# Seven added order constraints and one changed priority in the planner of an attention and two-MoE kernel

## The chip, the cores and the metric

The kernel runs on one core of a Trainium2 chip. Its engines are PE (the matmul array), DVE (vector), ACT (scalar), POOL (GpSimd) and SP, whose queue issues most of the DMAs. Each engine works through its own list of instructions in order, and waits at an instruction until what it needs is there. The metric is the device time of one execution in microseconds, and the time before is the median of 3 runs.

## The reference

Three stages follow each other. `B` is 4 batches, `H` 8 heads, `S` 576 tokens, `D` 64, `M` 32 memory slots.

```python
a = exp(phi - max(phi, axis=2)); a = a / (sum(a, axis=2) + 1e-09)     # over the 32 slots
k_m, v_m = einsum('bhsm,bhsd->bhmd', a, k), einsum('bhsm,bhsd->bhmd', a, v)
attn = softmax(q @ k_m.T / 8); x = (attn @ v_m), laid out as [2304 tokens, 512]

logits = x @ w_gate; e_idx = argmax(logits)                           # first MoE: 8 experts, one per token
out[mask_e] = gate_w * sigmoid(x @ w_output_gate)[:, e] * (relu(x @ w1[e]) @ w2[e])

p = domain_probs / (sum(domain_probs) + 1e-09)                        # second MoE: all 4 experts
out = sum_e p[:, e] * (relu(x @ w1[e]) @ w2[e])
```

## The kernel before

The attention is cut into eight units, u0 to u7: two of them (four heads each) per batch. A unit's steps have names that its instructions' lines tell: `ldph`, `ldkv`, `ldq` load phi, keys and values, and q; `mx` (lines 399 to 401, DVE) is the maximum over phi, `tr`, `gm`, `dg`, `pm` (L410, L417, L422, L426) turn it into one maximum per slot, `sub` (L432) subtracts it, `exp` (L440) follows on ACT, `es` on POOL and `pe` (L468) add up, `kva` and `kvb` (L449) are the products with keys and values, `r`, `kd`, `vd`, `vl` (L478 to L517) scale them, `ktT` (L502) and `kt` transpose, `sc0` and `sc1` (L569) are the scores, `t0` to `aT` (L594 to L634) the softmax, and `x0`, `x1` (L678) the output, which is split into a high and a low part (L686, L689 and others).

When both units of a batch are done, `route` (r0 to r3) computes the logits (L738), the largest one (`lz`), counts how many tokens chose each expert (`pc`, L812) and makes the most frequent expert's number (`idx`, lines 819 to 829, DVE). SP reads that number (`start`, L835, a TENSOR_LOAD) and loads that expert's weights (L1084). They are split on ACT (L1094) and DVE (L1102), and the dense matmuls of the first MoE begin (L942, then L950): batch 0's first one is the operation `m0a0`. From there on attention steps of later units stand between dense matmuls. Tokens that chose another expert are counted in `left` (L874) and would be handled in a general loop at the end. The second MoE (L1483, L1538) follows from about 300 us on, and its weights per token, `pr`, are loaded by `ld_probs` (L309, L313: 19 small DMAs in seven operations) and normalized by `probs` (L324 to L327, DVE).

What sets the order of all this up to the second MoE is a planner, `Plan`, which runs when the kernel is built. Each operation has an engine, an estimated cost, a priority (lower goes first), operations that it needs, and buffers that it takes. `run` steps through an imagined time, lets each engine take the ready operation of best priority, and writes its instructions at once, so that the order in which operations are taken becomes the order on each engine for good. An operation in `next` of another only has to be taken after that other one was; an operation in `succ` has to wait for its end. Until `m0a0` is taken, an idle PE is given `fill`, a 128 x 128 matmul of ones (L1361, named warm). Three of the lines that matter here:

```python
UNIT_PRIO = (158, 150, 200, 228, 230, 420, 656, 270)
        ld_probs.append(op(f"ld_probs{i0}", "S", 1.5, 650.0, [])(f))
    @op("probs", "V", 0.9, 1500.0, ld_probs)
```

Of the kernel before, what the change touches and what calls it, by code (L numbers as in the profile page):

```python
# [32 lines left out]
class Plan:  # L33
# [8 lines left out]
    def op(self, name, eng, cost, prio, after=(), take=()):  # L42
        def add(fn):
            o = Op(name, eng, cost, fn, prio, [(x,) if isinstance(x, str) else x for x in take])
            for a in after:
                if isinstance(a, tuple):
                    o.need += 1
                    a[0].next.append(o)
                elif a is not None:
                    o.need += 1  # L50
                    a.succ.append(o)
            self.ops.append(o)
            return o

        return add
# [101 lines left out]
def attn_moe_moe_kernel(  # L157
# [63 lines left out]
    left = const.tile([1, B], F32, name="left")  # L221
# [33 lines left out]
    plan = Plan(caps)  # L255
# [464 lines left out]
    def route(b, pri):  # L720
# [3 lines left out]
        def o(name, eng, cost, after=(), take=(), dp=0.0):  # L724
            return op(n0 + name, eng, cost, pri + dp, after, take)
# [115 lines left out]
        dp = 280.0  # L841
# [27 lines left out]
            T["pn"] = bank2(pn.got[0], "pn")[:, 0]  # L869
            nc.tensor.matmul(T["pn"][0:1, 0:1], T["ci"], ones[:P, 0:1], start=True, stop=True)  # L870

        @o("left", "V", 0.07, [pn], [], dp)
        def lf():
            nc.vector.tensor_scalar(left[:, b:b + 1], T["pn"][0:1, 0:1], -1.0, float(S), op0=ALU.mult, op1=ALU.add)  # L874

        plan.free(pn, 0, lf)

        @o("gate", "V", 2.12, [eo, oh], [], dp)
# [23 lines left out]
        def keep():  # L902
            nc.sync.dma_start(out=rs_d[b], in_=rest[b].rearrange("p j e -> p (j e)"))

        att_done.extend((start, gate, cb, lf, oh, eo))

    def w1_srcs(w1, e, nf):
# [512 lines left out]
    def first_w1(u, after, prev):  # L1420


        @op(f"n{u}t", "G", 3.6, pw_ - 500.0, [wraws_[2 * u], prev])
        def t():
            W0[u] = raw_tile(ts_p, "ts")
            for f in t_ops(wraws[(1, u)], W0[u]):
                f(nc.gpsimd)

        @op(f"n{u}h", "A", 2.2, pw_ - 500.0, [t, after])
        def h():  # L1430
            W1[u] = [big.tile([128, NP * 256], F32R, tag="xb", name="w") for _ in range(2)]
            for part in w1_parts(wraws[(1, u)], W0[u]):
                w1_hi(W1[u][0], part)

        @op(f"n{u}l", "G", 4.8, pw_ - 500.0, [h])
        def l():
            for part in w1_parts(wraws[(1, u)], W0[u]):
                w1_lo(nc.gpsimd, *W1[u], part)

        plan.free(wraws_[2 * u], 0, l)  # L1440
        return l

    n0l = first_w1(0, done_l1[2], None)
    first_w1(1, done_l1[3], n0l)
    plan.free(warm, 0, next(o for o in plan.ops if o.name == "m0a0"))
    plan.run()

    mctx.close()
# [190 lines left out]
```

## Time and profile before

| | |
|---|---|
| median of 3 runs | 1057.53 us (1056.83 to 1058.07) |
| profiled execution: its time, and its span | 1060.37 us, 1058.5 us |
| busy share of PE, DVE, POOL, ACT | 98%, 53%, 49%, 35% |
| granted PE clock, mean | 0.996 of full speed |
| first dense matmul (L942) | 54.94 us from the span's start |

The span is what the profiler saw between the first and the last instruction, and the time contains what lies around it as well. Busy time is what instructions take on an engine; a busy PE is not necessarily a PE at its full rate, which is why the granted clock is shown beside it.

### The profile page before, as it was taken

The numbers are of one execution on the slowest core, as the hardware profiler recorded it, in microseconds if no ns is written. First come the engines' busy times: TensorE is split into PE (matmuls) and PEld (weight loads), VectorE is DVE, ScalarE is ACT, GpSimd is POOL, SyncE is SP. The second block draws the span as 40 slices with busy tenths as digits, with TensorE's granted clock in tenths as the row PEclk, the third lists the DMA queues.
The fourth block names the chain that finished last, engine by engine and source line by source line (L and its number), as shares of the span: only waits on it lengthen the run. The fifth ranks groups of instructions, "written<-read, shape, count | busy, mean of one in ns | idle before, by whom it ended". The sixth has DMA issues, their size and how long they took to land.

```text
span 1058.5 us, 15693 instructions
## 1 busy us (share of the span) xinstructions
PE 1041.5 (98%) x6210; PEld 947.8 (90%) x6210; DVE 556.1 (53%) x1014; ACT 365.8 (35%) x610; POOL 519.3 (49%) x518
## 2 busy tenths in 40 slices
PE   8999999999999999999999999999999999999997
PEld 7879898999999999999998999999998999999996
DVE  4888876747334444545464454544456453453533
ACT  2343342424423243333243234333333323323330
POOL 1110110000447666766666665776666666666550
PEclk9999999999999999999999999999999999999999
DMA  9999883535442122212214212212214221221201
GB/s 197 171 237 183 156 256 79 184 89 185 136 144 80 45 76 80 65 56 80 80 50 129 80 40 81 80 47 74 80 51 129 80 69 51 80 80 40 60 20 63
DMA packets 137954, 104.93 MB, mean 99 GB/s; under 512 B 37008, under 2 KB 119952, under 8 KB 137872
## 3 DMA queue, kind: packets, MB, share of 16 engines
q1 hardware_dynamic: 137424, 102.66, 36.1%
q0 software_dynamic: 448, 1.19, 0.5%
q8 instruction: 50, 0.82, 0.3%
q14 instruction: 32, 0.26, 0.1%
HBM read 84.87 MB, written 18.96 MB: 98 GB/s over the span
## 4 chain that ended last, share of the span: by engine, by line
PE 91%; DMA 3%; DVE 3%; ACT 1%; SPq 1%; issue 0%
PE po L1538 37%; PE ab L1483 32%; PE p L942 9%; PE p L950 8%; DMA ph<-in_phi_dram 2%; DMA kv<-in_v_dram 1%; PE ub L449 1%; PE warm L1361 1%; PE px L678 1%; PE pss L569 1%; DVE l L1493 1%; PE pl L738 0%; DVE acc L1522 0%; PE pl L768 0%; ACT h L1492 0%
## 5 line engine op out<-in xcount | busy, mean ns | idle before, releaser
L1483 PE MATMUL ab<-zo,w 128*128 128x384 f32 x2004 | 401.4, 335 | 3.1 <-DVE zo L1286 3.1
L1483 PEld LDWEIGHTS ab<-zo,w 128*128 128x128 f32 x2004 | 356.2, 188 | 30.9 <-DVE zo L1286 3.7
L1538 PE MATMUL po<-w,h 128*128 128x512 f32 x1152 | 372.9, 391 | 0.3 <-ACT h L1492 0.3
L1538 PEld LDWEIGHTS po<-w,h 128*128 128x128 f32 x1152 | 214.4, 188 | 29.1 <-ACT h L1492 0.6
L1538 PE MATMUL po<-w,l 128*128 128x512 f32 x576 | 225.6, 392 | 0.0
L1344 POOL TENSOR_TENSOR w<-ts,w 128x512 fp32r<-128x512 f32 x92 | 118.4, 1308 | 127.3 <-ACT w L1568 127.3
L1492 ACT ACTIVATE h<-ab 128x384 fp32r<-128x384 f32 x143 | 70.3, 492 | 261.6 <-DVE ab L1514 170.9
L1344 POOL TENSOR_TENSOR w<-raw,w 128x512 fp32r<-128x512 f32 x100 | 102.8, 1050 | 112.9 <-ACT w L1340 112.9
L1493 DVE SCALAR_TENSOR_TENSOR l<-ab,h 128x384 fp32r<-128x384 f32 x143 | 79.8, 558 | 140.5 <-ACT h L1492 140.5
L1506 DVE TENSOR_TENSOR u<-ab,s 128x384 f32<-128x384 f32 x96 | 53.5, 558 | 150.9 <-PE ab L1483 119.0
L1573 POOL TENSOR_TENSOR w<-raw,w 128x512 fp32r<-128x512 f32 x96 | 123.9, 1310 | 16.4 <-ACT w L1563 16.4
L1538 PEld LDWEIGHTS po<-w,l 128*128 128x128 f32 x576 | 108.1, 188 | 16.6 <-DVE l L1493 0.3
L942 PE MATMUL p<-x,w 128*128 128x288 f32 x768 | 109.1, 299 | 0.0
L942 PEld LDWEIGHTS p<-x,w 128*128 128x128 f32 x768 | 104.0, 190 | 2.5 <-issue 2.1
L950 PE MATMUL p<-hh,w 128*128 128x288 f32 x512 | 93.6, 299 | 0.0
L1492 ACT ACTIVATE h<-t 128x384 fp32r<-128x384 f32 x48 | 25.2, 526 | 166.9 <-DVE t L1511 166.9
L1327 POOL TENSOR_TENSOR ts<-raw 128x256 f32<-128x256 f32 x92 | 81.8, 889 | 1.2 <-DMA raw<-in_moe_w_dram 1.2
L1493 DVE SCALAR_TENSOR_TENSOR l<-t,h 128x384 fp32r<-128x384 f32 x48 | 67.4, 1404 | 28.4 <-ACT h L1492 28.4
L950 PEld LDWEIGHTS p<-hh,w 128*128 128x128 f32 x512 | 76.2, 189 | 1.8 <-issue 1.7
L1327 POOL TENSOR_TENSOR ts<-raw,ts 128x256 f32<-128x256 f32 x92 | 68.7, 746 | 3.6
L1511 DVE TENSOR_TENSOR t<-ab,u 128x384 f32<-128x384 f32 x47 | 26.2, 557 | 62.5 <-PE ab L1483 62.5
L1514 DVE TENSOR_TENSOR ab<-ab,u 128x384 f32<-128x384 f32 x95 | 53.0, 558 | 6.5 <-PE ab L1483 6.4
(150 smaller groups left out, 906.3 us busy)
## 6 DMA issues: line engine op xcount, KB each, us to landing
raw<-in_moe_w_dram SPq DMA_DIRECT2D x79, 512.0 KB, 3.9
raw<-in_moe_w_dram SPq DMA_DIRECT2D x98, 256.0 KB, 4.3
xs<-x SPq DMA_DIRECT2D x16, 576.0 KB, 6.0
kv<-in_k_dram SPq DMA_DIRECT2D x16, 288.0 KB, 6.1
kv<-in_v_dram SPq DMA_DIRECT2D x16, 288.0 KB, 6.7
zs<-z SPq DMA_DIRECT2D x8, 576.0 KB, 5.2
ph<-in_phi_dram SPq DMA_DIRECT2D x8, 288.0 KB, 6.0
qt<-in_q_dram SPq DMA_DIRECT2D x16, 144.0 KB, 7.1
```

The costliest lines, as they stand in the source:

```text
L942: nc.tensor.matmul(pp[:, n, :HS], w[wi][:, kk, fs], zz[:, kk, n * HS:(n + 1) * HS], start=(kk == 0 and m == 0), stop=(kk == KD_ - 1 and m ...
L950: nc.tensor.matmul(pp[:, n, :HS], w[wi][:, j, :], hx[:, n * HS:(n + 1) * HS], start=(f == 0 and wi == 0 and hx is hh), stop=(f == NF - 1 a ...
L1327: lambda eng, o_=o_, x=x, y=y: eng.tensor_tensor(o_, x, y, op=ALU.subtract)
L1344: eng.tensor_tensor(wl[:, sl], src, wh[:, sl].bitcast(F32), op=ALU.subtract)
L1483: nc.tensor.matmul(p, w[:, s], z[:, zi, kk], start=(k not in (2, 3, 6) and kk + n == 0), stop=(kk == 1 and n == 2), skip_group_check=True,)
L1492: nc.scalar.activation(a, p, ACTF.Relu)
L1493: nc.vector.scalar_tensor_tensor(c, p, 0.0, a.bitcast(F32), op0=ALU.max, op1=ALU.subtract)
L1506: nc.vector.tensor_tensor(sums[n], p, sums["s1"], op=ALU.add)
L1511: nc.vector.tensor_tensor(t, p, sums["u3"], op=ALU.add)
L1514: nc.vector.tensor_tensor(p, p, sums["u3" if k == 5 else "u2"], op=ALU.add)
L1538: nc.tensor.matmul(po[t], hx[:, s], w[:, 1024 * wi + 512 * a:1024 * wi + 512 * a + 512], start=(i == 0 and a + n == 0), stop=(i == NI - 1 ...
L1573: nc.gpsimd.tensor_tensor(w[:, 1024:][:, c], wraws[(2, u)][:, c], w[:, c].bitcast(F32), op=ALU.subtract)
```

## The change

The priority of `left` goes from that of the rest of its group to the front, and seven pairs are added: the second name of each pair may be taken by the planner only after the first was. The pairs hold `u2mx` and the cast of the gates' weights (`gates`, L319 and L320) until `u1vd` has been taken, `u2sub` until `u1sb2`, `u3mx` until `u1aT`, `u4mx` until `r0idx`, the second q transpose of unit u1 until `u1pe`, and `r0pn` until `m0a0`. Costs, other priorities, buffers and the computation stay as they are.

```diff
@@ -869,7 +869,7 @@
-        @o("left", "V", 0.07, [pn], [], dp)
+        @o("left", "V", 0.07, [pn], [], -20.0)
         def lf():
@@ -1443,6 +1443,19 @@
     plan.free(warm, 0, next(o for o in plan.ops if o.name == "m0a0"))
+
+    named = {o.name: o for o in plan.ops}
+    for x, o in (
+        ("u1vd", "u2mx"),
+        ("u1vd", "gates"),
+        ("u1sb2", "u2sub"),
+        ("u1aT", "u3mx"),
+        ("r0idx", "u4mx"),
+        ("u1pe", "u1qt1"),
+        ("m0a0", "r0pn"),
+    ):
+        named[x].next.append(named[o])
+        named[o].need += 1
     plan.run()
```

The planner makes of it a different order from the second unit on. On DVE, around the index of route 0 (L819 to L829), there stood before (`lz`, `lmx`, `oh` are the logits, their maximum and the choice; `gm` and `dg` belong to units u3 and u4; `idx` is the expert's number):

```order
L751 TENSOR_REDUCE lz<-pl 96x96
L804 TENSOR_REDUCE lmx<-lz 96x6
L806 TENSOR_TENSOR oh<-lz,lmx 96x48
L417 TENSOR_REDUCE gm<-ub 128x1
L859 TENSOR_TENSOR dl<-lz,lmx 96x48
L422 TENSOR_SCALAR dg<-ident,gm 128x128
L417 TENSOR_REDUCE gm<-ub 128x1
L819 TENSOR_REDUCE cnt<-pc 128x8
L823 TENSOR_REDUCE cmx<-cnt 128x1
L825 SCALAR_TENSOR_TENSOR sel<-cnt,cmx,prio 128x8
L828 TENSOR_REDUCE cmx<-sel 128x1
L829 TENSOR_SCALAR idx_94<-cmx 1x1
```

Now there stands, at the same place:

```order
L804 TENSOR_REDUCE lmx<-lz 96x6
L806 TENSOR_TENSOR oh<-lz,lmx 96x48
L859 TENSOR_TENSOR dl<-lz,lmx 96x48
L324 TENSOR_REDUCE prs<-pr 128x18
L325 TENSOR_SCALAR prs<-prs 128x18
L326 RECIPROCAL prs<-prs 128x18
L327 TENSOR_TENSOR pr<-pr,prs 128x72
L819 TENSOR_REDUCE cnt<-pc 128x8
L823 TENSOR_REDUCE cmx<-cnt 128x1
L825 SCALAR_TENSOR_TENSOR sel<-cnt,cmx,prio 128x8
L828 TENSOR_REDUCE cmx<-sel 128x1
L829 TENSOR_SCALAR idx_94<-cmx 1x1
```

The steps of u3 and u4 have left this place, and the four instructions of `probs`, which before came after route 1, stand ahead of the counts. On SP, ahead of the read of the index (`TENSOR_LOAD idx`), before:

```order
L389 DMA ph<-in_phi_dram 96x4x192
L359 DMA qt<-in_q_dram 96x6x64 x2
L336 DMA kv<-in_k_dram 96x2x384
L337 DMA kv<-in_v_dram 96x2x384
L313 DMA pr<-in_moe_domain_probs_dram 96x4
L313 DMA pr<-in_moe_domain_probs_dram 32x4
L313 DMA pr<-in_moe_domain_probs_dram 64x4 x2
L313 DMA pr<-in_moe_domain_probs_dram 32x4
L313 DMA pr<-in_moe_domain_probs_dram 96x4
L352 DMA qd<-in_q_dram 32x18x32 x4
L835 TENSOR_LOAD idx_94
```

And now, at the same place:

```order
L313 DMA pr<-in_moe_domain_probs_dram 96x4 x2
L313 DMA pr<-in_moe_domain_probs_dram 32x4
L313 DMA pr<-in_moe_domain_probs_dram 64x4 x2
L313 DMA pr<-in_moe_domain_probs_dram 32x4
L313 DMA pr<-in_moe_domain_probs_dram 96x4
L309 DMA pr<-in_moe_domain_probs_dram 128x9x4
L336 DMA kv<-in_k_dram 96x2x384
L337 DMA kv<-in_v_dram 96x2x384
L359 DMA qt<-in_q_dram 96x6x64 x2
L835 TENSOR_LOAD idx_94
```

All 19 small loads of `pr` now come ahead of the read, in one row (before, 12 of them did, in two groups), and phi and the keys of u4 and the first q load of u4 have moved behind it. On PE, at the start of the dense matmuls (L942), before:

```order
L1361 MATMUL warm<-ones 128x128 x2
L449 MATMUL ub<-kv,ph 32x128 x12
L1361 MATMUL warm<-ones 128x128
L449 MATMUL ub<-kv,ph 32x128 x12
L1361 MATMUL warm<-ones 128x128 x2
L468 MATMUL ub<-ones,es 128x1
L1361 MATMUL warm<-ones 128x128 x2
L942 MATMUL p_807<-x,w 128x288 x24
L942 MATMUL p_855<-x,w 128x288 x12
L449 MATMUL ub<-kv,ph 32x128 x12
L942 MATMUL p_855<-x,w 128x288 x12
```

And now:

```order
L1361 MATMUL warm<-ones 128x128 x3
L426 MATMUL ub<-dg,ones 96x128
L1361 MATMUL warm<-ones 128x128 x9
L942 MATMUL p_785<-x,w 128x288 x24
L870 MATMUL pn<-ones,ci 1x1
L942 MATMUL p_826<-x,w 128x288 x12
L449 MATMUL ub<-kv,ph 32x128 x12
L942 MATMUL p_826<-x,w 128x288 x12
L449 MATMUL ub<-kv,ph 32x128 x12
```

The two L449 groups ahead of L942 before are those of u3, and the one behind it is u4's; now both groups behind L942 are u3's, and u4's come later. Ahead of the dense start stand 91 fillers, where 75 stood.

## Rows read from the trace of the kernel before

**Rows 1.** The page: share and instructions of PE; one kind of DMA issue, us to landing.

```profile
PE 1041.5 (98%) x6210; PEld 947.8 (90%) x6210; DVE 556.1 (53%) x1014; ACT 365.8 (35%) x610; POOL 519.3 (49%) x518
...
qt<-in_q_dram SPq DMA_DIRECT2D x16, 144.0 KB, 7.1
```

**Rows 2.** Table by stretches: length, busy us per engine, PE clock, DMA share, GB/s.

```profile
60.50:63.00 2.50, 0.03 (x2) 0.03 (x1) 1.67 (x3) 1.59 (x2) 0.00 (x0) 1.00 1.12 287
...
64.25:68.00 3.75, 3.75 (x36) 2.98 (x34) 2.85 (x6) 2.83 (x4) 0.00 (x0) 0.54 0.84 134
...
150.00:300.00 150.00, 150.00 (x1161) 145.34 (x1160) 84.96 (x159) 52.14 (x78) 19.33 (x20) 1.00 0.42 134
```

**Rows 3.** PE's timeline: start, us, instruction, count, idle before it and its releaser.

```profile
26.45 0.30 PE L410 MATMUL ub<-ident,mx 96*128 96x96 f32 x1 [1.15 <-DVE mx L401]
...
49.46 1.53 PE L1361 MATMUL warm<-ones 128*128 128x128 f32 x12
...
54.94 5.25 PE L942 MATMUL p<-x,w 128*128 128x288 f32 x36
...
63.01 0.85 PE L449 MATMUL ub<-kv,ph 96*32 96x128 f32 x20 [2.48 <-DMA kv<-in_v_dram]
```

**Rows 4.** SP's timeline of DMA issues: start, us until the last is issued, count.

```profile
31.58 1.24 SPq L359 DMA_DIRECT2D qt<-in_q_dram  x2
...
38.06 0.33 SPq L336 DMA_DIRECT2D kv<-in_k_dram  x1
...
51.02 3.50 SPq L1084 DMA_DIRECT2D raw<-in_moe_w_dram  x4
54.61 0.45 SPq L336 DMA_DIRECT2D kv<-in_k_dram  x1
...
96.83 5.61 SPq L313 DMA_DIRECT2D pr<-in_moe_domain_probs_dram  x6
```

**Rows 5.** The chain in order of time, 50 to 55 us: start, us, what.

```profile
50.99 0.42 PE ub L426 x2
...
51.87 0.79 PE ub L449 x24
...
54.51 0.13 PE ub L468 x2
```

**Rows 6.** SP's waits, 0 to 110 us: total, times, longest.

```profile
SPq L313 <- DMA qt<-in_q_dram: 1.6, 2, 1.2
```

**Rows 7.** Lines L313 and L309: ns of an issue (min/median/max); L309's landing.

```profile
L313 SPq DMA_DIRECT2D pr<-in_moe_domain_probs_dram x18: 317/490/1502, 32.9 to 102.0; - x18
...
DMA to landing us min/median/max: 2.7/2.7/2.7
```

**Rows 8.** DVE's timeline, columns as in PE's.

```profile
39.63 0.12 DVE L478 TENSOR_SCALAR rs<-ub 128x1 f32<-128x1 f32 x1
...
40.90 0.86 DVE L517 SCALAR_TENSOR_TENSOR vl<-ub,rm,vd 128x64 fp32r<-128x64 f32 x4
...
46.84 0.21 DVE L819 TENSOR_REDUCE cnt<-pc 128x8 f32<-128x48 f32 x1
...
47.74 0.14 DVE L829 TENSOR_SCALAR idx<-cmx 1x1 int32<-1x1 f32 x1
...
49.03 0.48 DVE L594 STREAM_TRANSPOSE t<-pss 128x288 f32<-128x288 f32 x1 [1.15 <-PE pss L569]
...
50.66 0.24 DVE L422 TENSOR_SCALAR dg<-ident,gm 128x128 f32<-128x128 f32 x1
...
70.72 0.20 DVE L846 TENSOR_TENSOR oh<-oh,prio 96x48 f32<-96x48 f32 x1
...
71.81 0.20 DVE L854 TENSOR_REDUCE ci<-inp 96x1 f32<-96x48 f32 x1
...
144.61 0.23 DVE L324 TENSOR_REDUCE prs<-pr 128x18 f32<-128x72 f32 x1
...
145.38 0.23 DVE L327 TENSOR_TENSOR pr<-pr,prs 128x72 f32<-128x72 f32 x1
```

## The prediction

> **What bounds the kernel now.** I read the page's shares first: PE is busy 98% of the span [rows 1]. So only three things can move the end: when the dense matmuls begin, how much other matmul work then shares PE with them, and the time PE stands still or runs slow behind that point. The table by stretches gives the last: from 150 to 300 us PE is busy throughout, while from 60.5 to 63 it is almost idle, and from 64.25 to 68 its granted clock averages 0.54 [rows 2]. PE's timeline names the places: the first dense matmul (L942) starts at 54.94, and at 60.5 the product of keys and values of the fifth unit, u4 (L449), waits 2.48 us for a kv load [rows 3]. That load was issued at 54.61, behind four loads of expert weights [rows 4]. After its 2.48 us of standing still PE fell from 2.4 to 1.2 GHz for most of 3.75 us; at 0.54 this cost 3.75 x 0.46 = 1.72 us.
>
> **What the change does, by engine.** The seven pairs only hold an operation back in the plan; at run time they add no wait themselves. But the plan is one program, so it shifts everything near the front.
>
> *PE behind the dense start.* Before, four units have their keys-and-values product ahead of the first L942 and five units their maxima; in the changed order it is three and four. One unit's two L449 groups (0.79 us each), an L426 (0.42), an L468 (0.13) and an L410 (no dearer than that; I take 0.08) move behind the start: 2 x 0.79 + 0.42 + 0.13 + 0.08 = **+2.2 us** [rows 5]. No cover: PE is full there.
>
> *The stall at 60.5.* Now the L449 behind 36 dense matmuls belongs to the fourth unit; its kv and q loads stand ahead of the expert weights in SP's order, issued at about 44 where PE needs them at about 61. I take the stall and its slow clock as gone: -2.48 - 1.72 = **-4.2 us**. Ends: 0 (it moves to another unit) and -4.2; the value taken is that of the kv load being early.
>
> *The dense start.* This is the uncertain term. The plan costs a `ld_probs` operation at 1.5 us, but its six small loads took 5.61 us on SP at 96.83 [rows 4]. The changed SP order issues all 19 before route 0's index is read, and the `probs` sums (L324 to L327), which wait for all of them, now stand on DVE directly ahead of the counts that make that index (L819 to L829). DVE is in order, so a normalization needed only hundreds of microseconds later sits in the chain that starts the dense work. Working forward:
> SP is unchanged up to the sixth small load. The seventh takes the place of the kv load at 38.06 [rows 4]. SP's small loads also wait for the end of earlier transfers, as for a q load [rows 6], but the last bulk load ahead of them is issued at 31.58 [rows 4] and lands within about 7 us [rows 1], so that from 39 on they run alone. A small load holds SP 0.49 us in the median [rows 7]: twelve from 38.06 give 38.06 + 11 x 0.49 = 43.45 for the issue of the last, and its landing took 2.7 us [rows 7]: 46.15. With the issue of the nineteenth I take **46.5**.
> DVE should be at L324 by about 44: it counted at 46.84 before, with the maxima of two more units ahead. So the landing decides.
> From 46.5: the four `probs` instructions, 144.61 to 145.61, 1.0; the five of the index, 46.84 to 47.88, 1.04; that is 48.55, against 47.88 before [rows 8]. Behind it the sums of the third unit, u2, kd, vd, vl (39.63 to 41.76, 2.13), six of the one-hot count (70.72 to 72.01, 1.29), two L594 (0.48 each, overlapping to about 0.4), L417 and L422 (0.24 each): 1.3 [rows 8]. This is 53.25; L426 on PE with its handover, 0.5; then nine fillers that stand in PE's order before L942, at 0.25 each (six, of two passes each, took 1.53 at 49.46 [rows 3]), 2.25. Together 48.55 + 2.13 + 1.29 + 1.3 + 0.5 + 2.25 = 56.0. The weights do not decide: their first load can issue at about 49.3, before 51.02 [rows 4]. So the start moves from 54.94 to 56.0: **+1.1 us**. Ends: if the loads land at 45 and DVE and PE keep step, -0.4; if each issue takes 5.61 / 6 = 0.94 us, the last is issued at 48.4, lands at 51.1, and the start moves +5.7.
>
> *Sum:* 2.2 - 4.2 + 1.1 = **-0.9 us**. On the profiled execution's span, 1058.5 becomes 1057.6. Its own time is 1060.37, 2.84 above the median of 1057.53; the same difference on the median gives **1056.6 us**. A change of 0.2% (2.1 us) is about what measurement tells from nothing here, so the forecast is no measurable change.
>
> **Rivals.**
> *The clock falls before the dense start (0.25).* In the changed order PE runs out of work at about 47.2 (fillers behind the last q transposes) and next needs the third unit's kd, some 0.8 us behind the index: 2.15 us idle. An idle of 1.15 us at 25.3 left the clock whole [rows 3], 2.48 us at 60.5 did not [rows 2, 3]. Half clock over the 2 to 4 us of PE's work ahead of L942 adds 1 to 2 us: sum +0.1 to +1.1, so 1057.6 to 1058.6. The Trainium skill, "TensorE: Matmul & The Clock Gate", Part 1 (the HAM clock gate), says that an idle array falls to half rate and needs sustained work to come back; by that rule the fillers pay, and the trace's fall at 64.25 agrees.
> *Slower: the small loads are slow (0.13).* At 0.94 us per issue the start moves +5.7 and the sum is +3.7: 1061.2. For it: 5.61 us for six at 96.83, and one issue of 1.50 us [rows 4, 7]; against it: those stood beside streams of q loads, and here no bulk runs. It decides (+2.1) once the last small load lands at 49.5 or later.
> *The stall stays (0.08).* The fourth unit's exponential stands on ACT behind the casts of the second and third weight pieces. If the third lands 2 us late, PE waits for it and its clock falls again: the 4.2 us come back, sum +3.3, 1060.8. For it: the exponential would end about 1 us before PE asks. Against: the weights are issued 1.7 us earlier with less ahead of them.
> *Faster: the loads are no wait (0.14).* If the 19 land by 44, the index is ready at 46 and the start at 53.5, sum -3.4: 1054.1. This is what the reordering by itself gives (two units' maxima off DVE ahead of the first softmax). For it: an issue can take 0.317 us [rows 7]: 11 x 0.32 from 38.06 is 41.6, landing 44.3. Against: back-to-back issues there took more.
>
> **How the numbers follow.** The forecast itself has 0.40. Faster by over 0.2%: all of the last rival, and 0.08 of the forecast for a landing near 45: 0.22. Slower: the slow loads, the stall that stays, and 0.03 of the clock rival: 0.24. The rest is 0.54. The range takes in both sides' cases, 1053.8 to 1061.2, leaving about 2 in 10 outside.
>
> **What would show it.** In the new trace: L324 waiting for a probs load, ending at 46 to 47; L829 at about 48.5; first L942 at 55.5 to 56.5; no L449 waiting for kv at 60 to 62; a granted clock of 1.00 from the start of L942 on; no PE wait over 1 us between 56 and 300. It is wrong if L324 ends before 45 or after 49.5, if the clock is at half when L942 begins, or if a new wait stands in the first 20 us of the dense work.

## The result: 1.4% slower, and the profile after

The changed kernel took 1074.64 us (median of 4 runs, 1071.10 to 1077.94); the kernel before, beside it on the same chip, 1057.80 (4 runs). The ratio is 1.0139, 95% interval 1.0114 to 1.0163. The profiled execution took 1077.94 us with a span of 1076.2 us, against 1060.37 and 1058.5: 17.7 us more span.

Four rows of PE's timeline answer to [rows 3] (start, us, instruction, idle before it and its releaser):

```profile
50.00 0.47 PE L502 MATMUL ub<-ident,kd 128*128 128x128 f32 x1 [1.84 <-DVE vl L517]
...
57.70 3.44 PE L942 MATMUL p<-x,w 128*128 128x288 f32 x24
...
91.53 0.59 PE L468 MATMUL ub<-ones,es 96*128 96x1 f32 x2 [6.36 <-POOL es L401]
...
153.14 0.42 PE L410 MATMUL ub<-ident,mx 96*128 96x96 f32 x1 [3.29 <-DVE mx L401]
```

The dense start is at 57.70, not 54.94. The wait for keys and values at 60.5 is gone, but two new ones stand behind the start: 6.36 us for u4's `es`, the sums that POOL makes, and 3.29 us for the maxima of u7. The table by stretches answers to [rows 2] (length, busy us of PE, PEld, which loads PE's weights, DVE, ACT and POOL, then PE clock, DMA share, GB/s):

```profile
50.00:54.00 4.00, 4.00 (x18) 2.42 (x18) 1.00 (x6) 0.89 (x3) 0.00 (x0) 0.60 0.92 302
57.70:85.10 27.40, 27.40 (x279) 24.83 (x277) 25.31 (x54) 13.69 (x20) 4.11 (x4) 1.00 1.13 188
85.10:91.50 6.40, 0.08 (x1) 0.00 (x0) 0.23 (x1) 0.00 (x0) 2.48 (x4) 0.67 1.02 162
91.50:99.00 7.50, 7.46 (x40) 7.47 (x41) 4.07 (x11) 0.96 (x2) 0.00 (x0) 0.60 1.10 295
149.80:153.20 3.40, 0.12 (x2) 0.06 (x1) 1.24 (x4) 0.00 (x0) 0.00 (x0) 0.85 1.08 324
153.20:162.00 8.80, 8.80 (x62) 7.37 (x63) 6.91 (x12) 3.23 (x5) 3.46 (x4) 0.67 0.51 190
```

Behind each idle stretch the granted clock is at its lower level, 1.2 of 2.4 GHz, for some microseconds: 7.50 x 0.40 = 3.0 us lost behind the first new wait, 8.80 x 0.33 = 2.9 us behind the second. These terms add up to nearly all of the 17.7: dense start 57.70 - 54.94 = 2.8; the deferred unit's work, 2.2 as forecast; 6.36 + 3.0 and 3.29 + 2.9 for the waits; 1.1 for two small waits at 271 and 275; less the 4.2 of before's own stall: 17.5. They compare one execution with one, not the medians.

The first new wait comes from an engine that the prediction never read. POOL's timeline before (its columns are those of PE's):

```profile
59.00 1.32 POOL L401 TENSOR_TENSOR es<-treeG 96x128 f32<-96x128 f32 x1
78.00 0.88 POOL L897 DMA_DIRECT2D cfd<-cf  x1 [17.68 <-DVE cf L891]
87.89 0.58 POOL L898 DMA_DIRECT2D cbc<-cfd  x1 [9.01 <-DMA cfd<-cf]
109.45 1.64 POOL L399 TENSOR_TENSOR treeG<-ph 96x384 f32<-96x384 f32 x1 [20.98 <-ACT ph L440]
```

And after:

```profile
63.37 0.65 POOL L401 TENSOR_TENSOR es<-treeG 96x128 f32<-96x128 f32 x1
74.11 0.88 POOL L897 DMA_DIRECT2D cfd<-cf  x1 [10.09 <-DVE cf L891]
88.83 0.58 POOL L898 DMA_DIRECT2D cbc<-cfd  x1 [13.84 <-issue]
89.42 1.00 POOL L399 TENSOR_TENSOR treeG<-ph 96x384 f32<-96x384 f32 x1
90.50 0.45 POOL L400 TENSOR_TENSOR treeG<-treeG 96x128 f32<-96x128 f32 x1
91.03 0.45 POOL L401 TENSOR_TENSOR es<-treeG 96x128 f32<-96x128 f32 x1
```

Before, u4's `es` (59.00) comes ahead of route 0's two gate DMAs: L897 writes 2.2 KB of gate values to memory, L898 reads them back to all partitions (the broadcast), and has to wait until they are there. After, `es` of u4 stands behind both (91.03 is u4's, 63.37 is u3's). Its input has been ready since ACT's exponential ended at 80.73, but POOL stands at L898 for 13.84 us, then needs 2.06 us for the three instructions of `es`, and PE, whose next instruction is L468, waits there. The planner had put the two DMAs at 6.0 us; from the start of L897 to the end of L898 they took 15.3 here (10.5 before). The orders on POOL differ at one more place, since route 1's broadcast now comes ahead of u5's `es` too, but no PE wait at L468 came of that in this kernel. The Trainium skill, "DMA: Bandwidth & Descriptors", section "Anatomy of one DMA", says that a DMA's wait on a semaphore is done by the sequencer that issues it; L898 agrees, with POOL held for 9.01 us before and 13.84 after. By the same section's fit (2.0 us and a term for bytes) 2.2 KB would land in about 2 us, which is an estimate; the view of DMA issues shows five times that, and the measurement decides (KB each, median us to landing):

```profile
cfd<-cf POOLq DMA_DIRECT2D x4, 2.2 KB, 10.2
```

### The profile page after: what moved, and what is told of

Same layout as the page of the kernel before. It is cut to its first block, busy times and chain, and to the rows that moved or that the text cites. A ratio compares the mean times of both kernels' runs of the same rounds, so it can differ in the third digit from the quotient of the medians.

```text
span 1076.2 us, 15760 instructions
## 1 busy us (share of the span) xinstructions
PE 1048.3 (97%) x6242; PEld 953.7 (89%) x6242; DVE 556.6 (52%) x1014; ACT 365.6 (34%) x610; POOL 518.4 (48%) x518
## 4 chain that ended last, share of the span: by engine, by line
PE 88%; DMA 3%; DVE 3%; SPq 2%; issue 2%; ACT 0%; POOL 0%; DVEq 0%; POOLq 0%
PE po L1551 36%; PE ab L1496 31%; PE p L950 9%; PE p L942 8%; DMA qt<-in_q_dram 1%; DMA cfd<-cf 1%; SPq L359 1%; DMA ph<-in_phi_dram 1%; PE pss L569 1%; PE ub L449 1%; SPq L313 1%; PE warm L1361 1%; PE px L678 1%; DVE l L1506 1%; DVE acc L1535 0%
## 5 line engine op out<-in xcount | busy, mean ns | idle before, releaser
L1519 DVE TENSOR_TENSOR u<-ab,s 128x384 f32<-128x384 f32 x96 | 53.5, 558 | 151.0 <-PE ab L1496 119.0
L942 PE MATMUL p<-x,w 128*128 128x288 f32 x768 | 113.3, 304 | 1.1 <-DVE z L1193 1.0
L942 PEld LDWEIGHTS p<-x,w 128*128 128x128 f32 x768 | 106.5, 194 | 5.5 <-issue 3.8
L897 POOL DMA_DIRECT2D cfd<-cf x4 | 3.2, 790 | 128.5 <-DVE cf L891 79.7
```

The source lines that it names most:

```text
L942: nc.tensor.matmul(pp[:, n, :HS], w[wi][:, kk, fs], zz[:, kk, n * HS:(n + 1) * HS], start=(kk == 0 and m == 0), stop=(kk == KD_ - 1 and m ...
L1519: nc.vector.tensor_tensor(sums[n], p, sums["s1"], op=ALU.add)
```

## The experiments

Theory 1: PE waits because POOL, in order, stands at route 0's broadcast with u4's `es` behind it; the half clock behind the wait is its consequence. Theory 2: u3 and u4 as a whole are too late, by the late dense start and by their held maxima, and this wait is only where it shows. Theory 3, for the second wait: SP's order issues u7's phi too late.

The results first. The span, the dense start, PE's idle time behind it and the time lost to the lower clock behind it (up to 300 us; summed over slices of 1 us of the table by stretches, the loss as busy time times one minus the clock) are of the one profiled execution.

| kernel | median, and before beside it | ratio, 95% | span | dense start | idle | lost to clock |
|---|---|---|---|---|---|---|
| before | 1057.80 | | 1058.5 | 54.94 | 3.1 | 1.7 |
| changed | 1074.64 / 1057.80 | 1.0139 (1.0114 to 1.0163) | 1076.2 | 57.70 | 11.3 | 5.9 |
| 1: es ahead of broadcast | 1068.76 / 1058.71 | 1.0077 (1.0054 to 1.0101) | 1069.4 | 60.65 | 5.2 | 1.7 |
| 2: before, es behind broadcast | 1066.03 / 1058.71 | 1.0062 (1.0035 to 1.0090) | 1064.2 | 56.17 | 6.7 | 3.4 |
| 3: probabilities later | 1071.30 / 1058.71 | 1.0104 (1.0073 to 1.0135) | 1071.4 | 53.53 | 10.2 | 6.9 |
| 4: only u3, u4 pairs | 1072.77 / 1058.71 | 1.0127 (1.0094 to 1.0160) | 1069.7 | 57.90 | 9.5 | 3.4 |
| 5: es and phi | 1066.69 / 1061.16 | 1.0060 (1.0037 to 1.0083) | 1064.1 | 54.73 | 5.3 | 3.4 |
| 6: es, phi, probabilities | 1063.58 / 1061.16 | 1.0035 (1.0014 to 1.0056) | 1059.8 | 53.25 | 4.7 | 0.0 |
| 7: broadcast planned at 15 | 1080.51 / 1061.16 | 1.0169 (1.0137 to 1.0200) | 1083.2 | 60.47 | 14.2 | 6.5 |
| 8: only u2 pairs | 1084.50 / 1061.16 | 1.0227 (1.0199 to 1.0256) | 1079.9 | 56.23 | 16.1 | 7.3 |
| 9: fillers ahead of L502 | 1075.73 / 1060.43 | 1.0146 (1.0104 to 1.0187) | 1070.7 | 56.22 | 10.8 | 2.2 |
| 10: fourth pair, z | 1065.63 / 1060.43 | 1.0048 (1.0022 to 1.0073) | 1063.6 | 53.72 | 6.5 | 1.7 |
| 11: before, u4's product held | 1069.58 / 1060.43 | 1.0080 (1.0053 to 1.0106) | 1063.8 | 56.01 | 7.3 | 2.5 |
| 12: before, kv load on ACT | 1061.55 / 1060.43 | 1.0008 (0.9983 to 1.0033) | 1064.0 | 59.22 | 4.4 | 1.7 |

One column has to be read with care. With the same instructions up to it, the dense start differs from execution to execution: 57.70, 60.65, 54.73 and 60.47 us in the changed kernel's order (changed, 1, 5, 7), 54.94, 56.17, 56.01 and 59.22 in that of before (before, 2, 11, 12). These ranges overlap, so a difference of 2.8 us between two executions says little of the medians.

**1. u4's `es` ahead of the broadcast.** The changed kernel with one more pair:

```diff
         ("m0a0", "r0pn"),
+        ("u4es", "r0cbc"),
```

> The changed kernel with one more pair: route 0's cbc (the two gate DMAs on POOL) may be taken only after u4's es. Every other queue keeps its order. Theory 1 (POOL's order): L401 of u4 no longer stands behind L898, the wait of 6.36 us at L468 and the 3.0 us of half clock behind it go, so about 9.4 us less: 1065 us. Theory 2 (u3 and u4 are late as a whole): another PE wait of 3 us or more takes the place of this one within 15 us, and the gain stays under 4 us: above 1070.

POOL's timeline and PE's, of this kernel:

```profile
85.55 0.46 POOL L401 TENSOR_TENSOR es<-treeG 96x128 f32<-96x128 f32 x1
85.95 0.88 POOL L897 DMA_DIRECT2D cfd<-cf  x1
97.93 0.58 POOL L898 DMA_DIRECT2D cbc<-cfd  x1 [11.10 <-DMA cfd<-cf]
```

```profile
50.14 0.47 PE L502 MATMUL ub<-ident,kd 128*128 128x128 f32 x1 [1.98 <-DVE vl L517]
...
60.65 1.56 PE L942 MATMUL p<-x,w 128*128 128x288 f32 x10
...
146.88 0.30 PE L410 MATMUL ub<-ident,mx 96*128 96x96 f32 x1 [3.18 <-DVE mx L401]
```

The broadcast waits as long as ever (11.10 us), but nothing of PE's stands behind it: no wait at L468 is left, nor its half clock, and no wait over 0.6 us took its place until the one at 146.88. Theory 2 asked for one of 3 us within 15 us, and falls for this wait. Only POOL's order differs from the changed kernel's, at this one place. The median fell by 5.9 us, the ratio from 1.0139 to 1.0077, with intervals that do not overlap: less than the 9.4 expected. In the profiled execution half clock ahead of the dense start lasted much longer (60.65 against 57.70 with the same instructions up to there); why the median gained less is not shown.

**2. The swap alone, in the kernel before.**

```diff
+    named = {o.name: o for o in plan.ops}
+    for x, o in (
+        ("r0cbc", "u4es"),
+    ):
+        named[x].next.append(named[o])
+        named[o].need += 1
     plan.run()
```

> The kernel before with one pair: u4's es may be taken only after route 0's cbc. None of the seven pairs of the change is in it, and the way to the dense start is the same. Theory 1: route 0's broadcast ends near 88.5 us, es ends near 90.6, PE is at L468 near 84.5, so a wait of about 6 us and some 3 us of half clock: 9 us or more slower than before, 1066 to 1072. Theory 2 (the swap is harmless without late u3 and u4): within 2 us of before.

```profile
61.13 1.35 PE L449 MATMUL ub<-kv,ph 96*32 96x128 f32 x24
...
86.91 0.38 PE L468 MATMUL ub<-ones,es 96*128 96x1 f32 x2 [2.29 <-POOL es L401]
...
130.95 0.38 PE L468 MATMUL ub<-ones,es 96*128 96x1 f32 x2 [1.68 <-POOL es L401]
```

PE's timeline shows the wait, twice (the planner then put route 1's broadcast ahead of u5's `es` too), each with half clock behind it; the kernel is 7.3 us slower by the medians. None of the change's pairs is needed for the wait. It is smaller than expected, since the first broadcast came 4 us earlier here (L898 at 83.83). Not all of the 7.3 us is the swap's: the planner moved later work too, and three waits for `hl` (the low part of the hidden layer, L962) of 2.6 us together stand at 262 to 271. One thing more: the old wait at 60.5 is not in this execution (L449 at 61.13), although PE, DVE, ACT and SP have the same order as before up to there.

**3. The sums over the probabilities later.** They leave the chain that makes the index:

```diff
+        ("m0a0", "probs"),
```

> The changed kernel with one more pair: the sums over the probabilities (L324 to L327) only after m0a0, so that the index of route 0 no longer waits for the last small load. Theory 1: the dense start moves from 57.7 to about 55 and PE does not fall to half clock ahead of it, but the wait at L468 stays, since POOL's order is as in the changed kernel: 1 to 3 us less, 1072. Theory 2 (the late dense start is what makes the rest late): the L468 wait shrinks under 3 us and the time falls by 8 us or more, under 1067.

```profile
53.53 3.43 PE L942 MATMUL p<-x,w 128*128 128x288 f32 x24
...
87.57 0.59 PE L468 MATMUL ub<-ones,es 96*128 96x1 f32 x2 [4.02 <-POOL es L401]
```

The dense start came 4.2 us earlier than in the changed kernel, and even 1.4 earlier than before, with the clock whole. Yet the wait at L468 stays (4.02), behind POOL's same order (here the profile names the write: L898 waits 12.08 us for `cfd`), and the ratio falls by 0.35% only, with intervals that overlap. The start is a cost by itself; it is not what makes the rest late.

**4. Only the pairs for u3 and u4**, `("u1aT", "u3mx")` and `("r0idx", "u4mx")`, in the kernel before.

> The kernel before with two of the seven pairs (u1aT ahead of u3mx, r0idx ahead of u4mx). u3 and u4 come later, but on POOL u4's es stays ahead of route 0's broadcast. Theory 1: no wait at L468 over 1 us, within 3 us of before (1055 to 1061). Theory 2 (late u3 and u4 are the cost): 5 us or more slower, above 1063.

Neither theory's account. There is no wait at L468, as Theory 1 says, and the time is where Theory 2 put it, 1.3% slower, but for another reason: PE's and DVE's timelines show one long wait elsewhere. The dense start is late as well (57.90), behind a wait of 2.99 us for a q load at 52.07.

```profile
139.00 0.47 PE L502 MATMUL ub<-ident,kd 128*128 128x128 f32 x1 [7.62 <-DVE vl L517]
```

```profile
133.39 0.78 DVE L539 STREAM_TRANSPOSE qq<-qd 128x576 f32<-128x576 f32 x1 [8.49 <-DMA qd<-in_q_dram]
```

DVE stood 8.49 us at a copy of q, in order, with the sums of u5 (L478 to L517), for which PE waited, behind it. It is an event of the same kind on another engine. In the changed kernel these two pairs do nothing: the planner gives the same order on every engine without them.

**5. `es` and phi.** Experiment 1 with one more pair:

```diff
+        ("u4es", "r0cbc"),
+        ("u7ldph", "u6ldkv1"),
```

> The kernel of the first run (u4's es ahead of route 0's broadcast) with one more pair: u6's second load of keys and values only after u7's load of phi, so that on SP phi of u7 no longer waits behind two loads that hold SP for 3.5 us. Theory 3 (SP's order makes the second stall): phi is issued 3 us earlier, the wait of 3.18 us at L410 falls under 1 us and its 1.8 us of slow clock go: 4 to 5 us less than the first run, 1064. Rival (phi's buffer comes free too late whatever the order): the issue moves by under 1 us and the time by under 1.5 us.

SP's timeline and PE's:

```profile
130.36 1.70 SPq L389 DMA_DIRECT2D ph<-in_phi_dram  x1
132.10 0.48 SPq L336 DMA_DIRECT2D kv<-in_k_dram  x1
```

```profile
139.39 0.30 PE L410 MATMUL ub<-ident,mx 96*128 96x96 f32 x1 [1.64 <-DVE mx L401]
```

The wait halves, 3.18 to 1.64. Phi is issued 1.8 us earlier than in experiment 1, counted from the dense start (130.36 - 54.73 = 75.6 against 138.06 - 60.65 = 77.4), not 3: SP is held 1.70 us at it. Half of Theory 3 is right; the rest is that the load lands 7.8 us after its issue (DVE's L399 at 138.13). A wait of 3.0 us for z (L1193, the first MoE's output times its gate) also came up at 258. By the ratio it gains 0.17%, within both intervals.

**6. `es`, phi and probabilities**: the three pairs of 3 and 5 together.

> The changed kernel with three more pairs: u4's es ahead of route 0's broadcast, u7's phi ahead of u6's second load, the sums over the probabilities after m0a0. If the three waits are the whole cost, the sum against before is: dense start 53.5 for 54.9 (-1.4), the deferred unit's work +2.2, the stall and slow clock of before -4.2, a late wait near 263 us +1.2: -2.2, so 1055 to 1058, at or under before. If the late second to fourth units are themselves the cost, new PE waits of 3 us or more come up and it stays above 1062.

1.0035 of before, not at or under it as expected. Against the profile of before: start -1.7, deferred work +2.2, idle +1.6, clock -1.7, so +0.4 of the 1.3 us more span. The pairs undo three quarters of the loss. They don't leave a gain: in this execution the dense start won is paid back by the unit's work that it leaves behind, and small waits (1.63 at L410, 0.94 at L449, 1.2 at L942) remain.

**7. The broadcast planned at 15 us.**

```diff
-        @o("cbc", "G", 6.0, [gate], ["cbc"], dp)
+        @o("cbc", "G", 15.0, [gate], ["cbc"], dp)
```

> The changed kernel with the planner's cost of a route's broadcast at 15 us in place of 6. The order on POOL stays (broadcast of route 0 ahead of u4's es), but the planner now puts L468 of u4 9 us later on PE, behind other work. Theory 1, in the form that the planner's 6 us hide the real 14.7: the wait at L468 falls under 1 us with POOL's order as it was, 6 to 9 us less, 1066 to 1069, if the later routes do no worse. Theory 2: the wait only moves with the chain of u4 and the gain is under 3 us.

POOL's order is that of the changed kernel, and L468 does not wait: PE comes to it 38.6 us behind the dense start (99.08 - 60.47), where it came after 27.4 us in the changed kernel, and there the order does no harm, as Theory 1 has it. But the 6 to 9 us less did not come. The whole is 1.7% slower than before, since the planner moved much else, and at 148.01 stands a new wait:

```profile
99.08 0.28 PE L468 MATMUL ub<-ones,es 96*128 96x1 f32 x2
...
148.01 1.21 PE L449 MATMUL ub<-kv,ph 96*32 96x128 f32 x20 [4.25 <-DMA kv<-in_v_dram]
```

**8. Only the pairs for u2** (`u2mx`, `gates`, `u2sub`, `u1qt1`), without the new priority of `left` and the pair for `r0pn`.

> The kernel before with four of the seven pairs, those that hold u2mx, the gates' cast, u2sub and u1's second q transpose; not the pairs for u3mx and u4mx and not the new priority of left. The planner's order on POOL is already that of the changed kernel (route 0's broadcast ahead of u4's es). Theory 1: the wait at L468 is there, 4 us or more, and the time is 1067 or more. Theory 2 (the pairs for u3 and u4 do it): no wait at L468 over 1 us and under 1062.

A miss for both. It has the changed kernel's order on POOL, but no wait for u4's `es` (L468 at 87.15; a wait of 0.79 at 61.89 is for u3's), and is slower than the changed kernel. The planner put u3's steps directly behind one another on PE:

```profile
65.34 0.33 PE L502 MATMUL ub<-ident,kd 128*128 128x128 f32 x1 [2.09 <-DVE vd L495]
...
80.01 0.85 PE L678 MATMUL px<-S,vd 128*128 128x288 f32 x2 [4.76 <-DVE x L689]
```

From 61 to 80 it waits at nearly every step of that chain, much of the rest at half clock. POOL's order is harmful only where PE's order asks for `es` early; a part of the change can be worse than the whole. The pairs for u3 and u4 do nothing here either, so the rest of the change, `left` and `r0pn` together, takes back 0.9% (1.0227 to 1.0139); what each of the two does was not run.

**9. Fillers where PE is idle ahead of the dense start**, in the changed kernel:

```diff
+            for _ in range(6 if u == 2 else 0):
+                fill()
             nc.tensor.transpose(T["ub"][:, 384:512], T["kd"].rearrange("p a d -> p (a d)"), ident)
```

> The changed kernel with six more fillers ahead of u2's L502, where PE stands idle 1.84 us before the dense start; all other orders stay. If that idle is what sends the clock to half, the granted clock from 50 to 54 us is 1.00 and the dense start moves from 57.7 to 55 or 56, 2 to 5 us less: 1070 to 1072, with less spread between executions. Rival (the clock falls for another reason): clock at half there as before, no gain.

PE's timeline (L504 and L944 are L502 and L942, two lines further down) and the stretch that answers to 50 to 54 above:

```profile
49.93 0.33 PE L504 MATMUL ub<-ident,kd 128*128 128x128 f32 x1 [0.82 <-DVE vl L519]
...
56.22 3.42 PE L944 MATMUL p<-x,w 128*128 128x288 f32 x24
```

```profile
50.00:54.00 4.00, 4.00 (x31) 2.73 (x31) 2.20 (x10) 1.45 (x4) 0.00 (x0) 1.00 0.94 283
```

With 0.82 us of idle in place of 1.84 the clock stays at 1.00 and the dense start comes 1.5 us earlier; the wait at L468 is still there (5.86). The time shows no gain (1.0146, whose interval holds the changed kernel's). What this front costs in the median is therefore not shown, only what it costs in an execution.

**10. A fourth pair, `("m2y3", "zsS1")`**, on top of 6.

> The kernel with the three added pairs (es, phi, probs) and a fourth: the first sum over z for the second MoE (L1274) only after the last L1193 of route 2, so that on DVE L1193 no longer stands behind a wait of 6 us for a DMA. PE's wait of 1.2 us near 254 goes: 1.2 us less than without it, 1.0015 to 1.003 of before. Rival: the wait moves to the start of the second MoE, no gain or a loss of 2 us.

No gain: the wait near 254 went (the sum at L1274 now comes later), but 1.9 us for `hl` stand at 262 in its place.

**11. The forecast's -4.2 by itself**: the kernel before with `("m0b1", "u4kva")` and `("u5es", "r1cbc")`.

> The kernel before with two pairs: u4's first keys-and-values product only after the fourth group of dense matmuls (m0b1), and route 1's broadcast only after u5's es so that POOL's order stays that of before. It measures the term that the prediction put at -4.2 by itself: with 2 us more of dense work ahead of it the wait at 60.5 falls under 1 us and PE keeps its clock, -3 to -4 us: 1054. If the planner's other moves bring a new PE wait of 3 us or more, it ends above 1058.

The wait at 60.5 is gone, but the planner moved u7's phi, SP stood 7.39 us at its issue, and PE waits 5.53 us for it at 143.59. The term could not be had alone, and the time cannot price it.

**12. u4's second load of keys and values from ACT's queue**, in the kernel before.

```diff
-            nc.sync.dma_start(out=t[:, 0], in_=k[b, hs].rearrange("h (p j) d -> p h j d", j=NJ))
-            nc.sync.dma_start(out=t[:, 1], in_=v[b, hs].rearrange("h (p j) d -> p h j d", j=NJ))
+            q = nc.scalar if (u, i) == (4, 1) else nc.sync
+            q.dma_start(out=t[:, 0], in_=k[b, hs].rearrange("h (p j) d -> p h j d", j=NJ))
+            q.dma_start(out=t[:, 1], in_=v[b, hs].rearrange("h (p j) d -> p h j d", j=NJ))
```

> The kernel before with u4's second load of keys and values issued by ACT in place of SP; no order is changed by the planner. If SP's order (four loads of weights ahead) is why PE waits 2.48 us at 60.5, the load is issued about 52.7 in place of 54.6, the wait falls under 1 us and the slow clock goes: 2 to 4 us less, 1054 to 1056. Rival (the DMA engines are full there): issued earlier it lands as late, no gain; and ACT, which waits for the buffer, delays the casts of the weights: 0 to 2 us more.

No change that can be told. ACT, in order too, came to the issue at 58.45, behind casts of weights; the wait was 1.59, with the clock whole behind it, in an execution whose dense start was 59.22. Whether SP's order or the full DMA engines (share 1.12 in [rows 2]) made the old stall stays open.

## Why the prediction was wrong

It forecast 1056.6 us, range 1053.8 to 1061.2, and gave slower by over 0.2% a chance of 0.24; the time was 1074.64.

**The step that failed** is the list of what waits behind the dense start: "no PE wait over 1 us between 56 and 300". The prediction followed PE, DVE, ACT and SP across the change and left out POOL. The two orders on POOL differ in when `es` comes against the gate DMAs: u4's against route 0's, and u5's against route 1's. The first made the largest cost, 6.36 us and 3.0 of clock. Experiments 1, 2 and 7 show it: without the swap no wait, with the swap alone in the old kernel the wait, though smaller (2.29), and with PE's step later the swap without harm. The prices stood in the trace of before: the landing wait of 9.01 us (and 12.79 for route 1) at L898, which the planner costs at 6.0 with the write.

**The dense start, +1.1, was +2.8** from this execution to that of before. The mechanism was as said: L324 waited for a probs load and ended at 46.14 (forecast 46 to 47), L829 came at 47.72 (48.5). (The loads are four operations, three of six and one of one, not the seven named ahead of the prediction; its sum reckons with six.)

```profile
45.91 0.23 DVE L324 TENSOR_REDUCE prs<-pr 128x18 f32<-128x72 f32 x1 [2.28 <-DMA pr<-in_moe_domain_probs_dram]
...
47.72 0.14 DVE L829 TENSOR_SCALAR idx<-cmx 1x1 int32<-1x1 f32 x1
...
54.24 0.48 DVE L594 STREAM_TRANSPOSE t<-pss 128x288 f32<-128x288 f32 x1 [3.10 <-PE pss L569]
```

From there it was forecast to take 7.4 us and took 10.0. Two things were missing. The sum held DVE's work between u2's `vl` and L594 but not PE's and ACT's (L502, `kt`, L569), for which DVE waited 3.10 us. And the clock rival, given 0.25, came in: 1.84 us idle at 48.16, then 0.60 of full clock from 50 to 54. Where the clock stayed whole with the same instructions (experiment 5) L829 to L942 took 54.73 - 46.17 = 8.6 us, so 1.1 of the missing 2.5 is the first and 1.4 the second. Experiment 3 confirms the cause: with the sums out of the chain the start is at 53.53, as the "faster" rival's 53.5, and 6 and 10, which hold the sums back too, have it at 53.25 and 53.72, ahead of all eight starts listed under the table.

**The stall at 60.5** is gone, as forecast: from 57.70 to 85.10 PE is busy throughout at 1.00. What replaced it was not in the two places where the prediction looked (u3's exponential, the small loads). But its price, -4.2, was read in one execution of the kernel before and taken off the median, and that execution was 2.84 us above the median. In experiment 2, with the same order up to there on every engine but POOL, the stall is not there at all, and in experiment 12 it was 1.59 us with no half clock. What the term is worth in the median is not shown, and may be well under 4.2.

**The deferred work, +2.2,** was not measured alone; with it the sums for the changed kernel and experiments 1, 3, 5 and 6 (start, idle, clock against before) come within 1 us of the span's difference.

**The second wait, 3.29 + 2.9 us,** was in no rival. SP's order made half of such a wait (experiment 5); behind the other half stands a load of phi that lands 7.8 us after its issue. Why it lands so late, and what each cause is worth in the median, stays open.

## What to carry to other kernels

When a planner reorders a program, read the order of every engine that issues or waits, the quiet ones above all: a DMA that waits for another one holds up all that stands behind it in that engine's order, here for 9 to 15 us. Price such a pair at what the trace shows (15.3 us here, 6.0 in the plan) and ask of each instruction behind it when PE will want it. In this kernel, where PE's order is full, one long wait cost half to nearly as much again through the clock (3.0 behind 6.36, 2.9 behind 3.29), and undoing one wait by a planner's rule often made another elsewhere (experiments 4, 7, 10 and 11). And before a stall is taken off a median, look whether more than one execution has it.

## What the runs showed of the hardware

Whether the clock fell after an idle stretch of 1.3 to 2.0 us differed. At the same place ahead of the dense start PE kept its full clock after 1.32 and 1.67 us of idle (experiments 5 and 8) and fell to half after 1.84, 1.98 and 2.04 (changed, 1, 7); at u7's L410 it kept it after 1.63 (6) and fell after 1.64 and 1.48 (5, 10). How long half clock then lasted differed with the same instructions: some 4 us in the changed kernel, 10 in experiment 1, whose dense start is 2.95 us later for it. The Trainium skill, "TensorE: Matmul & The Clock Gate", Part 1, says of the ramp at a kernel's start that it differs from run to run of one kernel; these rows, from the middle of a kernel, show the like. The clock goes with the spread of the times: the six executions of experiment 1 go from 1064.83 us at a mean clock of 0.999 to 1071.16 at 0.992.

After a write of 2.2 KB from POOL's queue the read behind it stood 7 to 15 us until it could go: for route 0 9.01 before, and 11.10 and 14.28 in experiments 1 and 6, while the DMA engines' share was 0.9 to 1.0. Full DMA engines are not the whole of it: for route 2 of the kernel before the read stood 8.20 us while the share was 0.19 (171.3 to 180.3), and the shortest of all, 7.21 (experiment 1, route 1), had a share of 0.32. What makes up these 7 to 8 us no run shows. In the changed kernel the profile names only "issue" for the 13.84.
